# A fused attention and feed-forward kernel: the later pairs' queries and keys are split into high and low parts, stacked to 128 rows and projected with the whole array

## The chip, the core and the metric

The kernel runs on one core of one Trainium2 chip. The metric is the device time of one execution in microseconds (us); the time that stands for a kernel is the median of its timed runs. A difference under 0.2% of this kernel's time, some 2.3 us, is about what a measurement cannot tell from no change. Engines: PE (TensorE) runs the matmuls, PEld its weight loads, DVE is VectorE, ACT is ScalarE, POOL is GpSimd, SP is the queue from which nearly all transfers start.

## The reference

```python
def _attn_ref(q, k, v, w_phi):                       # q, k, v: 8 x 8 x 576 x 64, w_phi: 64 x 128
    def phi(x):
        proj = np.einsum('bhsd,df->bhsf', x, w_phi)
        proj = proj - np.max(np.abs(proj), axis=-1, keepdims=True)
        return np.concatenate([np.exp(proj), np.exp(-proj)], axis=-1)
    q_p, k_p = (phi(q), phi(k))
    kv = np.einsum('bhsf,bhsd->bhfd', k_p, v)
    z = np.sum(k_p, axis=2)
    num = np.einsum('bhsf,bhfd->bhsd', q_p, kv)
    den = np.einsum('bhsf,bhf->bhs', q_p, z)[..., None] + 1e-06
    return num / den

def _moe_ref(x, w_gate, w_val, w_out):               # x: 4608 x 512, inner width 1536
    g = x @ w_gate
    return (g * (1 / (1 + np.exp(-g))) * (x @ w_val)) @ w_out
```

The output of the attention, laid out as 4608 tokens by 512, is the x of the feed-forward part. All inputs are float32.

## The kernel before

**Work.** The 64 heads are 32 pairs of heads (`NPAIR` 4 to a batch entry, `i` counts them); the function `attention(i, rank)` adds one pair's steps. The first 12 pairs (`EARLY_PAIRS`) go through an early form, the other 20, called the later pairs here, through a second form. The tokens of the feed-forward part are 12 chunks of 384 (`CH`). The first 4 chunks use plain products (`first`, `second`), the other 8 are taken two at a time by Strassen's scheme (`operands`, `strassen`), whose operands are sums of quarters; those run from about 475 us on, and the first of them needs the later pairs' results.

**Precision.** Feed-forward products take float32 numbers as a high part, rounded to the type float32r, and a low part, the rest, and run three matmuls (high x high, high x low, low x high) in float32r; `matmuls` at line 389 and `prod` at line 1214 issue them, with 128 rows and 128 stationary columns each. The projections of attention use plain float32: one matmul of the program is two weight loads and two matmuls in the trace.

**Projection of a later pair.** A pair's keys lie as 64 rows for head 0 above 64 rows for head 1 in the tile `kin`, queries in `qin`, and `w_phi` lies twice, once for each half, in `wst`. A matmul takes 64 rows only, so the two heads' matmuls use the two halves of the array side by side (this is mode "rows" in the planner). For keys the tile of 128 tokens is stationary and `wst` moves; for queries `wst` is stationary and 288 tokens move:

```python
nc.tensor.matmul(work[plan.bank["k", i, h]][:, t * NF:(t + 1) * NF],          # 562
                 kin[rows(h)[0], t * P:(t + 1) * P], wst[rows(h)[0]], ...)
nc.tensor.matmul(work[plan.bank[keys[h]]][:, :SH], wst[rows(h)[0]],           # 705
                 qin[jq][rows(h)[0], c], ...)
```

Line 565 projects the last 64 tokens of both heads. What follows on keys (`L573`, `L579`, `L584`) makes their exponentials, `L601` and `L594` sum keys times values (called kv below), `L710` copies the queries out of PSUM, `L714` to `L742` make their exponentials, and `L760` multiplies them with the sums (called nu below). kv and nu use 64 columns of the array (mode "columns").

**Order.** Nothing is ordered by hand. Each step is added to a `Plan` with a cost, predecessors and a rank; `Plan.run` plays all engines forward with these costs, picks the next step of each engine, hands out the 8 PSUM banks, and issues in that order, so each engine's order is fixed when the kernel is built. `pe32(n)` is its cost for a pair of float32 projections, `pe(n)` for a float32r matmul, and 165 ns (`CHANGE`) are added where PE's mode changes. When PE has nothing ready, `nothing` issues an idle matmul of 128 x 256 (`L1413` and, before the feed-forward part begins, `L1411`).

**Weights.** `weight_piece` turns the float64 weights into high and low parts in 36 pieces, over scratch tiles `raw`, `we`, `wa`, which are slices of one tile `shared`. The later pairs' `turned` results reuse the room of `raw` when the weights are done.

Of the kernel before, what the change touches and what calls it, by code (L numbers as in the profile page):

```python
# [285 lines left out]
def favor_attention_moe(ctx: ExitStack, tc: tile.TileContext, qT, kT, v, w_phi, wg, wv, wo, out):  # L286
# [195 lines left out]

    turned = lambda n: later("turned", "shared", [P, 2, 2, 2, SH], F32)[:, n]

# [31 lines left out]
    def attention(i, rank):  # L516
# [8 lines left out]
        k_in = [add("SP", P * 4 * P * 4, lambda: nc.sync.dma_start(kin[:, :4 * P], kT[b, pr, :, :4 * P]),  # L525
                    [last.get(("kin", i - 1))], rank)]
        side = lambda t: t[:D, 4 * P:].rearrange("d (h s) -> d h s", h=2)
        ends = lambda t: t[b, pr, :, 4 * P:].rearrange("(h d) s -> d h s", h=2)
        k_in.append(add("SP", 2 * D * D * 4, lambda: nc.sync.dma_start(side(kin), ends(kT)), [last.get(("kin", i - 1))], rank))
        q_free = [last.get(("qin", n)) for n in ((i - 2,) if early else (i - 1, i - 2))]  # L530
        q_width = 4 * P if early else S
# [12 lines left out]

        kv_steps, summed, made_keys = [], [], []
        ps_kv = lambda: work[plan.bank["kv", i]]
        for g, (t0, t1) in enumerate(K_GROUPS):
# [9 lines left out]
            def project(t0=t0, t1=t1, key=key, heads=heads, both=both):  # L557
                projected.append(1)
                if not both:
                    for t in range(4):  # L560
                        for h in range(2):
                            nc.tensor.matmul(work[plan.bank["k", i, h]][:, t * NF:(t + 1) * NF],  # L562
                                             kin[rows(h)[0], t * P:(t + 1) * P], wst[rows(h)[0]], start=True, stop=True)
                if both or not early:
                    nc.tensor.matmul(work[plan.bank["k", i, 2]][:, :NF], kin[:D, 4 * P:], wst[:D], start=True, stop=True)  # L565

            if both and early:
                kproj = add("PE", pe32(NF), project, [*k_in, kproj], rank, take=key, mode="rows")
            elif not g:
                kproj = add("PE", (4 if early else 5) * pe32(NF), project, [*k_in, last.get(("kp", i - 1, 0))], rank,  # L570
                            take=[("k", i, n) for n in range(2 if early else 3)], mode="rows")
            m = km[(3 * i + g) % len(km)]
# [49 lines left out]
        last["kin", i] = kproj  # L622
        last["vf", i] = kv_steps[-1]
# [16 lines left out]
        if early:  # L640
            for g in range(3):
# [51 lines left out]
                f1 = add("ACT", act(size), lambda f=exponential: f(1), [f0, *([f1] if g else ())], rank, give=key2)  # L693
            last["qin", i] = pj
            if jq:
                ahead_used.append(pj)
        else:
            copies = [[], []]
            pj = None
            for part, c in enumerate(halves):  # L700
                keys = [("q", i, h, part) for h in range(2)]

                def project(keys=keys, c=c):
                    for h in range(2):
                        nc.tensor.matmul(work[plan.bank[keys[h]]][:, :SH], wst[rows(h)[0]], qin[jq][rows(h)[0], c],  # L705
                                         start=True, stop=True)

                pj = add("PE", pe32(SH), project, [*q_in, pj, *use("qx"), last.get(("qy", 3 * i - 1))], rank, take=keys, mode="rows")
                for h in range(2):
                    copies[h].append(add("ACT", act(SH), lambda h=h, part=part, key=keys[h]: nc.scalar.copy(  # L710
                        qx[j][:, h].rearrange("p (n u s) -> p u n s", u=2, s=32)[:, part],
                        work[plan.bank[key]][:, :SH].rearrange("p (n s) -> p n s", s=32)), [pj, *use("qx")], rank, give=keys[h]))
            last["qin", i] = pj
            turns = [add("DVE", dve(S), lambda h=h: vec.transpose(qe[j][:, h], qx[j][:, h]),  # L714
# [657 lines left out]
    for f in range(NFT):  # L1372
        sums(f)
    bring()
    behind = [(c, f) for c in (1, 2) for f in range(NFT)]
    coming.extend([*behind, *((PLAIN - 1, f) for f in range(NFT))])
# [89 lines left out]
```

## Time and profile before

| | |
|---|---|
| time, median of 3 runs | 1163.08 us (1162.91 to 1163.36) |
| the profiled execution, its own time | 1161.04 us |
| its span in the trace | 1159.2 us |
| busy PE | 1152.4 us, 99% |
| busy PEld | 1015.2 us, 88% |
| busy DVE | 793.7 us, 68% |
| busy ACT | 546.7 us, 47% |
| granted TensorE clock | full in every slice of the table |

Busy PE counts the overlapping, modelled ends of pipelined matmuls, and idle matmuls too, so 99% says that PE always has something in flight and not that it is at its peak. How long a matmul holds PE is read from a run of them: the time from the first to the start of what follows, divided by their number. The chain of waits lists PE that way. The DVE and ACT shares are means over stages that differ.

### The profile page before, as it was taken

Reading aid. Unit: us, or ns where it says so; the run is one execution under the profiler, and the core shown is the slowest. Engines: PE = TensorE matmul, PEld = TensorE weight load, DVE = VectorE, ACT = ScalarE, POOL = GpSimd, SP = SyncE. Lnnn points to the kernel's source line nnn. Section 1 sums busy time; section 2 is a strip of 40 time slices with the busy share of each in tenths; the row PEclk is TensorE's granted clock in tenths of the full one; section 3 lists DMA queues with packets and bytes.
Section 4 is the critical chain, followed back from the end, with each engine's and each line's share of the span. In section 5 each row is a group of like instructions: output and inputs, shape, how many; then the busy total and the mean of one; then the engine's idle time right before and its main releaser. Section 6 shows DMA issues by size and latency. Waiting matters only on the chain.

```text
span 1159.2 us, 26379 instructions
## 1 busy us (share of the span) xinstructions
PE 1152.4 (99%) x9985; PEld 1015.2 (88%) x9985; DVE 793.7 (68%) x1573; ACT 546.7 (47%) x1233; POOL 139.6 (12%) x142
## 2 busy tenths in 40 slices
PE   9999999999999999999999999999999999999998
PEld 8777779999898888898987899898899998899986
DVE  7989899999567777477787455777536786534431
ACT  6887563333434555445455343554423553433332
POOL 1222300000122313010010001100001100001100
PEclk9999999999999999999999999999999999999999
DMA  5546678777799999997887788887888787889774
GB/s 170 178 144 197 220 254 289 249 261 263 268 313 297 326 298 359 340 307 233 243 281 235 252 274 288 239 255 245 264 267 272 246 248 232 270 284 304 246 222 159
DMA packets 220591, 298.32 MB, mean 257 GB/s; under 512 B 65840, under 2 KB 126384, under 8 KB 220464
## 3 DMA queue, kind: packets, MB, share of 16 engines
q1 hardware_dynamic: 220304, 296.57, 79.7%
q8 instruction: 79, 1.29, 0.5%
q14 instruction: 48, 0.39, 0.1%
q10 hardware_dynamic: 160, 0.07, 0.0%
HBM read 217.91 MB, written 78.64 MB: 256 GB/s over the span
## 4 chain that ended last, share of the span: by engine, by line
PE 86%; DVE 1%; DMA 1%; issue 0%; SPq 0%; ACT 0%; ACTq 0%
PE work L389 41%; PE work L1214 31%; PE work L760 4%; PE work L601 4%; PE work L705 2%; PE work L562 2%; PE work L594 1%; PE work L1413 1%; DMA w_lo<-wlo_dram 0%; DMA stage<-x_dram 0%; PE work L565 0%; PE work L817 0%; PE work L813 0%; PE work L677 0%; DVE qy L667 0%
## 5 line engine op out<-in xcount | busy, mean ns | idle before, releaser
L389 PE MATMUL work<-w_hi,hh 128*128 128x512 f32 x468 | 183.1, 399 | 0.0
L1236 DVE TENSOR_TENSOR m<-m,work 128x384 f32<-128x384 f32 x144 | 78.6, 552 | 117.7 <-ACT m L1233 67.8
L389 PE MATMUL work<-w_hi,m 128*128 128x512 f32 x396 | 156.7, 396 | 0.0
L382 DVE TENSOR_TENSOR m<-m,hh 128x384 fp32r<-128x384 f32 x132 | 74.8, 573 | 97.7 <-ACT hh L1002 85.8
L1002 ACT CAST hh<-m 128x384 fp32r<-128x384 f32 x144 | 73.3, 512 | 138.5 <-PE work L389 74.2
L389 PE MATMUL work<-xh,w_big 128*128 128x384 f32 x384 | 132.3, 345 | 0.0
L382 POOL TENSOR_TENSOR m<-m,m 128x384 f32<-128x384 f32 x48 | 58.7, 1223 | 590.5 <-DVE m L1241 296.1
L389 PE MATMUL work<-xl,w_big 128*128 128x384 f32 x384 | 128.6, 335 | 0.0
L1214 PE MATMUL work<-tb,stream_xh 128*128 128x384 f32 x618 | 115.3, 338 | 0.0
L1214 PEld LDWEIGHTS work<-tb,stream_xh 128*128 128x128 f32 x618 | 107.0, 188 | 4.7 <-issue 3.8
L389 PEld LDWEIGHTS work<-w_hi,hh 128*128 128x128 f32 x468 | 87.9, 188 | 21.5 <-issue 1.7
L1233 ACT COPY m<-work 128x384 f32<-128x384 f32 x144 | 68.0, 475 | 73.2 <-PE work L1214 71.0
L1240 ACT ACTIVATE m<-m 128x384 f32<-128x384 f32 x96 | 45.5, 517 | 110.2 <-DVE m L1236 109.5
L584 ACT ACTIVATE kp<-kp 128x512 f32<-128x512 f32 x128 | 78.5, 630 | 26.5 <-DVE kp L579 25.3
L389 PEld LDWEIGHTS work<-w_hi,m 128*128 128x128 f32 x396 | 74.4, 188 | 17.8
L1214 PE MATMUL work<-tb,stream_xl 128*128 128x384 f32 x468 | 88.9, 338 | 0.4 <-ACT m L1233 0.4
L1214 PEld LDWEIGHTS work<-tb,stream_xl 128*128 128x128 f32 x468 | 81.0, 188 | 4.0 <-issue 2.3
L389 PEld LDWEIGHTS work<-xh,w_big 128*128 128x128 f32 x384 | 72.2, 188 | 7.5 <-issue 4.4
L1214 PE MATMUL work<-tb,tb 128*128 128x384 f32 x408 | 77.8, 337 | 0.0
L601 PEld LDWEIGHTS work<-vf,kp 128*64 128x64 f32 x2048 | 62.6, 138 | 13.4 <-issue 5.5
L382 POOL TENSOR_TENSOR s<-s 128x256 f32<-128x256 f32 x48 | 41.3, 862 | 270.1 <-DMA s<-w_dram 231.7
L389 PEld LDWEIGHTS work<-xl,w_big 128*128 128x128 f32 x384 | 72.2, 188 | 1.0
(141 smaller groups left out, 2340.1 us busy)
## 6 DMA issues: line engine op xcount, KB each, us to landing
stream_xh<-wv_dram SPq DMA_DIRECT2D x103, 256.0 KB, 4.0
h_dram<-m SPq DMA_DIRECT2D x124, 192.0 KB, 3.8
m<-h_dram SPq DMA_DIRECT2D x124, 192.0 KB, 4.1
stream_xl<-wv_dram SPq DMA_DIRECT2D x78, 256.0 KB, 3.9
tb<-wv_dram SPq DMA_DIRECT2D x77, 256.0 KB, 4.1
w_lo<-wlo_dram SPq DMA_DIRECT2D x72, 256.0 KB, 4.2
stream_w_lo<-wv_dram SPq DMA_DIRECT2D x52, 256.0 KB, 3.9
stream_xl<-wlo_dram SPq DMA_DIRECT2D x48, 256.0 KB, 3.8
```

The lines of the kernel that those rows point to most:

```text
L382: (nc.gpsimd if on == "POOL" else nc.vector).tensor_tensor(out=o, in0=a, in1=b, op=op)
L389: nc.tensor.matmul(o, l, r, start=a, stop=z)
L562: nc.tensor.matmul(work[plan.bank["k", i, h]][:, t * NF:(t + 1) * NF], kin[rows(h)[0], t * P:(t + 1) * P], wst[rows(h)[0]], start=True, st ...
L584: nc.scalar.activation(kpv[:, :m2, s], kpv[:, :m2, 1], AF.Exp, scale=-1.0 if s else 1.0)
L601: nc.tensor.matmul(ps_kv()[r, (2 * s + h) * VD:(2 * s + h + 1) * VD], kpv[:, t, s, r], vf[:, t, h], start=t == 0 and h + s == 0, stop=False)
L705: nc.tensor.matmul(work[plan.bank[keys[h]]][:, :SH], wst[rows(h)[0]], qin[jq][rows(h)[0], c], start=True, stop=True)
L760: nc.tensor.matmul(o[r, at:at + VD], features(k, h, slice(D * n, D * n + D)), kvs[j][:, (2 * k + h) * VD:(2 * k + h + 1) * VD], start=n % ...
L1002: s4 = add("ACT", act(CH), lambda: nc.scalar.copy(hh[b], th(j)), [made, hid_free[b]], FIRST)
L1214: nc.tensor.matmul(o(), l, r, start=begin and k + m == 0, stop=k + m == 3, skip_group_check=True)
L1233: return j, into(j, add("ACT", act(CH), lambda: nc.scalar.copy(th(j), src()), after, FIRST))
L1236: return add("DVE", dve(CH), lambda: vec.tensor_tensor(out=th(j), in0=th(j), in1=src(), op=ALU.add), after, FIRST)
L1240: s1 = into(t, add("ACT", act(CH), lambda: nc.scalar.activation(th(t), th(j), AF.Tanh, scale=0.5), [ready], FIRST))
```

## The change

The 20 later pairs' projections get another form. `w_phi` is split once into a high part `w_hi_phi` and a low part `w_lo_phi`. For each head of a later pair, ACT rounds the head's 64 rows to float32r into one half of a 128-row tile (`stack`), and DVE writes what is left over into the other half. One matmul over the 128 rows then multiplies high and low parts with `w_hi_phi`, a second adds their product with `w_lo_phi`. Each head's four key tiles fill one PSUM bank, and each half of a head's queries is a step with a bank of its own. The scratch tiles of the weights become six tiles, and the stacks take the room of `we` and `wa`.

```diff
+    w_parts = sb("w_hi_phi", [P, NF], F32R), sb("w_lo_phi", [P, NF], F32R)
...
-    shared = pool.tile([P, 4, 2 * DM], F32, name="shared", tag="shared")
-    shared = [shared[:, i].bitcast(dt) for i, dt in enumerate((U32, U32, F32, F32))]
-    raw = [t.rearrange("p (n t) -> p n t", t=2) for t in shared[:2]]
-    we, wa = ([t[:, i * DM:(i + 1) * DM] for i in range(2)] for t in shared[2:])
+    raw = [t[:, :2 * DM].rearrange("p (n t) -> p n t", t=2) for t in sb("raw", [P, 2 * S], U32, 2)]
+    we = [sb("we0", [P, 4 * P])[:, :DM], sb("we1", [P, S])[:, :DM]]
+    wa = [sb("wa0", [P, KW])[:, :DM], sb("wa1", [P, S])[:, :DM]]
...
+    STACKS = {"k1": ("we0", 4 * P), "q0": ("we1", S), "k0": ("wa0", KW), "q1": ("wa1", S)}
...
+    def split_phi():
+        hi = add("ACT", act(NF), lambda: nc.scalar.copy(w_parts[0], wst), (), EARLY_PAIRS - 0.5)
+        phi_parts.append(add("DVE2", dve(NF), lambda: nc.vector.tensor_tensor(
+            out=w_parts[1], in0=wst, in1=w_parts[0], op=ALU.subtract), [hi], EARLY_PAIRS - 0.5))
+    def stacked(name, h, src, n, after, rank):
+        own, other = rows(h)
+        free = [*wa_free, *we_free]
+        hi = add("ACT", act(n), lambda: nc.scalar.copy(stack(name)[own, :n], src[own, :n]), [*after, *free], rank)
+        return [hi, add("DVE2", dve(n), lambda: nc.vector.tensor_tensor(
+            out=stack(name)[other, :n], in0=src[own, :n], in1=stack(name)[own, :n], op=ALU.subtract), [hi], rank)]
...
+            def project_whole(g=g, t0=t0, t1=t1, key=key, both=both):
+                projected.append(1)
+                for t in range(t0, t1) if both else range(4):
+                    o = work[plan.bank[key]][:, :NF] if both else work[plan.bank[key]][:, t * NF:(t + 1) * NF]
+                    for n, w in enumerate(w_parts):
+                        nc.tensor.matmul(o, stack("k0" if both else f"k{g}")[:, t * P:(t + 1) * P], w, start=n == 0, stop=n == 1)
+            if not early:
+                kproj = add("PE", (1 if both else 4) * 2 * pe(NF), project_whole,
+                            [*key_parts[g % 2], *phi_parts, last.get(("kp", i - 1, g))], rank, take=key)
...
-                pj = add("PE", pe32(SH), project, [*q_in, pj, *use("qx"), last.get(("qy", 3 * i - 1))], rank, take=keys, mode="rows")
+                    def project(h=h, at=at, ps_q=ps_q):
+                        for n, w in enumerate(w_parts):
+                            nc.tensor.matmul(ps_q(), w, stack(f"q{h}")[:, at], start=n == 0, stop=n == 1)
+                    pj = add("PE", 2 * pe(SH), project, [*parts_of[h], *phi_parts, *use("qx"), last.get(("qy", 3 * i - 1))],
+                             rank, take=key)
```

What this does to the issued order is seen at three places. The first is PE in the first Strassen stage, at a later pair's queries. Before (L705 the query projections, two heads side by side; L1214 feed-forward products):

```order
L705 MATMUL work_131<-qin,wst 128x288
L705 MATMUL work_134<-qin,wst 128x288
L1214 MATMUL work_127<-tb_4973,stream_xh_5354 128x384 x6
L1214 MATMUL work_133<-tb_5018,stream_xh_5041 128x384 x3
L705 MATMUL work_130<-qin,wst 128x288
L705 MATMUL work_132<-qin,wst 128x288
L1214 MATMUL work_133<-tb_5018,stream_xh_5041 128x384 x3
```

In the change, at the like place (L740 the new query projections, L1248 the former L1214):

```order
L1248 MATMUL work_136<-tb_5168,stream_w_lo1v 128x384 x3
L740 MATMUL work_139<-stack_q_3458,w_hi_phi 128x288
L740 MATMUL work_139<-stack_q_3458,w_lo_phi 128x288
L1248 MATMUL work_136<-tb_5168,stream_w_lo1v 128x384 x3
L740 MATMUL work_137<-stack_q_3458,w_hi_phi 128x288
L740 MATMUL work_137<-stack_q_3458,w_lo_phi 128x288
L1248 MATMUL work_140<-tb_5261,tb_5252 128x384 x6
```

Two steps of two 64-row matmuls became four steps of two 128-row matmuls, each between products. In the whole order the later pairs' 80 matmuls of L705 become 160, and their 180 of L562 and L565 become 360 of a new line 591; the idle matmuls of L1413 go from 67 to 56; all feed-forward matmuls are the same in number.

The second place is PE where a later pair's kv (L601, L594) and another's nu (L760) stand, in the same stage. Before:

```order
L1214 MATMUL work_129<-tb_4973,stream_xh_5041 128x384 x6
L601 MATMUL work_131<-vf,kp_101 64x65 x16
L601 MATMUL work_131<-vf,kp_102 64x65 x16
L594 MATMUL work_131<-vl,kpt 64x130 x4
L760 MATMUL work_134<-kvs_104,qe_108 64x65 x2
L760 MATMUL work_134<-kvs_104,qx_106 64x65 x2
```

In the change (L631 and L624 are kv, L794 is nu):

```order
L631 MATMUL work_134<-vf,kp_103 64x65 x16
L631 MATMUL work_134<-vf,kp_104 64x65 x16
L624 MATMUL work_134<-vl,kpt 64x130 x4
L1248 MATMUL work_140<-tb_5252,stream_w_lo1v 128x384 x6
L1248 MATMUL work_136<-tb_5168,tb_5252 128x384 x6
L1248 MATMUL work_140<-tb_5261,tb_5252 128x384 x6
L794 MATMUL work_139<-kvs_106,qe_110 64x65 x2
```

Products of 128 columns now stand between the two. Counted over the 20 later pairs, kv and nu stand next to each other 14 times before and 6 times in the change. Of the 40 steps of L705 before, 34 have products on both sides and 6 stand next to another attention block; the 20 key blocks stand apart from kv and nu.

The third place is DVE in the same stage, behind the subtraction of the query maxima (L738 before, L772 in the change). Before:

```order
L735 STREAM_TRANSPOSE qe_108<-peaks 128x576 x2
L738 TENSOR_TENSOR qx_106<-qx_106,qe_108 128x576 x2
L573 TENSOR_REDUCE km_113<-work_131 128x4
L573 TENSOR_REDUCE km_114<-work_134 128x4
L579 TENSOR_TENSOR kp_101<-work_131,km_113 128x4x128
L1236 TENSOR_TENSOR m_5898<-m_5898,work_133 128x384
```

In the change (L499 are the new low parts, L1270 is the former L1236):

```order
L772 TENSOR_TENSOR qx_109<-qx_109,qe_111 128x576
L499 TENSOR_TENSOR stack_k_3431<-kin,stack_k_3431 64x640
L499 TENSOR_TENSOR stack_k_3439<-kin,stack_k_3439 64x512
L499 TENSOR_TENSOR stack_q_3445<-qin,stack_q_3445 64x576
L499 TENSOR_TENSOR stack_q_3458<-qin,stack_q_3458 64x576
L772 TENSOR_TENSOR qx_109<-qx_109,qe_111 128x576
L1270 TENSOR_TENSOR m_5705<-m_5705,work_135 128x384
```

All four subtractions of a pair stand together here, ahead of L1270, which empties PSUM banks of the products; elsewhere they come one or two at a time.

## Rows read from the trace of the kernel before

**Rows 1.** The page: engines, busy us, share of the span, instructions.

```profile
PE 1152.4 (99%) x9985; PEld 1015.2 (88%) x9985; DVE 793.7 (68%) x1573; ACT 546.7 (47%) x1233; POOL 139.6 (12%) x142
```

**Rows 2.** Chain of waits, long runs: start us, us, what.

```profile
460.13 2.75 PE work L1413 x23
...
999.97 17.48 PE work L389 x75
1017.45 85.48 PE work L1214 x492
```

**Rows 3.** Chain of waits in the first Strassen stage: start us, us, what.

```profile
541.14 2.10 PE work L760 x72
543.24 1.79 PE work L1214 x9
545.02 0.69 PE work L705 x4
545.71 1.79 PE work L1214 x9
547.50 0.69 PE work L705 x4
548.18 4.91 PE work L1214 x27
553.09 1.09 PE work L562 x16
554.18 0.22 PE work L565 x2
554.40 10.63 PE work L1214 x60
565.03 2.02 PE work L601 x64
567.04 0.44 PE work L594 x8
567.49 2.10 PE work L760 x72
569.59 1.79 PE work L1214 x9
```

**Rows 4.** Chain of waits at 414 us: a nu block alone.

```profile
414.62 2.25 PE work L760 x72
```

**Rows 5.** Timeline of PEld behind mode changes: start us, us, operation, count.

```profile
482.97 0.30 PEld L1214 LDWEIGHTS work<-tb,stream_w_lo 128*128 128x128 f32 x2
```

**Rows 6.** Groups by line and form: count, busy us, mean ns of one, idle before.

```profile
L1214 PEld LDWEIGHTS work<-tb,stream_xh 128*128 128x128 f32 x618 | 107.0, 188 | 4.7 <-issue 3.8
...
L738 DVE TENSOR_TENSOR qx<-qx,qe 128x576 f32<-128x576 f32 x40 | 29.8, 773 | 0.0
...
L740 ACT ACTIVATE qe<-qx 128x576 f32<-128x576 f32 x40 | 27.0, 683 | 11.6 <-DVE qx L738 11.2
...
L430 ACT CAST w_big<-shared 128x512 fp32r<-128x512 f32 x24 | 14.9, 621 | 15.5 <-DVE shared L382 15.2 <-POOL shared L382 0.2
...
L382 DVE TENSOR_TENSOR w_lo<-shared,w_hi 128x512 fp32r<-128x512 f32 x7 | 4.8, 687 | 0.0
```

**Rows 7.** Windows, three stretches with later pairs: busy us and instructions of each engine.

```profile
480.00:600.00 120.00, 120.00 (x1316) 108.53 (x1316) 88.24 (x184) 60.30 (x141) 12.39 (x10) 1.00 0.85 271
720.00:800.00 80.00, 80.00 (x882) 72.44 (x881) 64.18 (x133) 42.64 (x97) 8.46 (x7) 1.00 0.85 259
880.00:960.00 80.00, 80.00 (x780) 72.38 (x780) 60.05 (x123) 40.78 (x95) 9.08 (x8) 1.00 0.80 249
```

**Rows 8.** Windows of line 562 alone: PE and PEld busy us (records, 16 for a pair).

```profile
480.00:600.00 120.00, 6.97 (x96) 5.83 (x96) 1.00 0.85 271
720.00:800.00 80.00, 3.49 (x48) 2.91 (x48) 1.00 0.85 259
```

**Rows 9.** Tile `shared`: engine, operation, count, ns min/median/max, first and last start us.

```profile
L430 ACT CAST w_hi<-shared x12: 603/622/629, 62.9 to 295.2; 128x512 fp32r<-128x512 f32 x12
```

**Rows 10.** Chain of waits: the keys of the first two later pairs.

```profile
187.48 1.09 PE work L562 x16
...
342.25 1.09 PE work L562 x16
```

More of the change, by code (lines that the diff above doesn't have):

```diff
@@ L545, in attention @@
         kv_steps, summed, made_keys = [], [], []
+        if not early:
+            key_parts = [stacked(f"k{h}", h, kin, (KW, 4 * P)[h], [*k_in, *last.get(("keys", i - 1, h), ())], rank) for h in range(2)]
         ps_kv = lambda: work[plan.bank["kv", i]]
@@ L563, in project @@
                                              kin[rows(h)[0], t * P:(t + 1) * P], wst[rows(h)[0]], start=True, stop=True)
-                if both or not early:
+                if both:
                     nc.tensor.matmul(work[plan.bank["k", i, 2]][:, :NF], kin[:D, 4 * P:], wst[:D], start=True, stop=True)
-            if both and early:
+            def project_whole(g=g, t0=t0, t1=t1, key=key, both=both):
[4 more added lines that the diff above has]
+                        nc.tensor.matmul(o, stack("k0" if both else f"k{g}")[:, t * P:(t + 1) * P], w, start=n == 0, stop=n == 1)
+            if not early:
+                kproj = add("PE", (1 if both else 4) * 2 * pe(NF), project_whole,
+                            [*key_parts[g % 2], *phi_parts, last.get(("kp", i - 1, g))], rank, take=key)
+                last.setdefault(("keys", i, g % 2), []).append(kproj)
+            elif both:
                 kproj = add("PE", pe32(NF), project, [*k_in, kproj], rank, take=key, mode="rows")
             elif not g:
-                kproj = add("PE", (4 if early else 5) * pe32(NF), project, [*k_in, last.get(("kp", i - 1, 0))], rank,
-                            take=[("k", i, n) for n in range(2 if early else 3)], mode="rows")
+                kproj = add("PE", 4 * pe32(NF), project, [*k_in, last.get(("kp", i - 1, 0))], rank,
+                            take=[("k", i, n) for n in range(2)], mode="rows")
             m = km[(3 * i + g) % len(km)]
@@ L621, in attention @@
                 last["kp", i, g] = kv_steps[0]
-        last["kin", i] = kproj
+        last["kin", i] = [kproj] if early else [key_parts[h][1] for h in range(2)]
         last["vf", i] = kv_steps[-1]
@@ L693, in attention @@
                 f1 = add("ACT", act(size), lambda f=exponential: f(1), [f0, *([f1] if g else ())], rank, give=key2)
-            last["qin", i] = pj
+            last["qin", i] = [pj]
             if jq:
@@ L698, in attention @@
             copies = [[], []]
[L699 to L706, printed above, removed]
-                pj = add("PE", pe32(SH), project, [*q_in, pj, *use("qx"), last.get(("qy", 3 * i - 1))], rank, take=keys, mode="rows")
-                for h in range(2):
-                    copies[h].append(add("ACT", act(SH), lambda h=h, part=part, key=keys[h]: nc.scalar.copy(
+            parts_of = [stacked(f"q{h}", h, qin[jq], S, [*q_in, *last.get(("stack", i - 1, h), ())], rank) for h in range(2)]
+            last["qin", i] = [parts_of[h][1] for h in range(2)]
+            for h in range(2):
+                last["stack", i, h] = []
+                for part in range(2):
+                    at = slice(part * SH, part * SH + SH)
+                    key = ("q", i, h, part)
+                    ps_q = lambda key=key: work[plan.bank[key]][:, :SH]
+                    def project(h=h, at=at, ps_q=ps_q):
[3 more added lines that the diff above has]
+                             rank, take=key)
+                    last["stack", i, h].append(pj)
+                    copies[h].append(add("ACT", act(SH), lambda h=h, part=part, ps_q=ps_q: nc.scalar.copy(
                         qx[j][:, h].rearrange("p (n u s) -> p u n s", u=2, s=32)[:, part],
-                        work[plan.bank[key]][:, :SH].rearrange("p (n s) -> p n s", s=32)), [pj, *use("qx")], rank, give=keys[h]))
-            last["qin", i] = pj
+                        ps_q().rearrange("p (n s) -> p n s", s=32)), [pj, *use("qx")], rank, give=key))
             turns = [add("DVE", dve(S), lambda h=h: vec.transpose(qe[j][:, h], qx[j][:, h]),
@@ L1374, in favor_attention_moe @@
     bring()
+    split_phi()
     behind = [(c, f) for c in (1, 2) for f in range(NFT)]
```

10 lines of the change are left out of this document (6 added, 4 removed).

## The prediction

> **What bounds the kernel now.** I read the page first, then the chain of waits, then groups and windows. The page shows PE in flight for 99% of the span and no other engine above 68% [rows 1]; this says only where to look, since a busy PE may be issuing idle matmuls or waiting for its weights. The chain tells what a matmul costs in a run. 492 feed-forward matmuls of 128 x 384 take 85.48 us, 0.1737 each; 75 of 128 x 512 take 17.48 us, 0.233 each; 23 idle ones of 128 x 256 take 2.75 us, 0.1196 each [rows 2]. In the Strassen stage products and attention blocks follow each other without a break: the run of 60 products behind a key block takes 10.63 us, and 60 times 0.1737 is 10.42 [rows 3]. The 0.2 us left over stands in every such run between two attention blocks (9 products take 1.79 where 9 times 0.1737 is 1.56), however long the run, so it is the price of leaving and entering the 128 x 128 mode, and not a wait. What PE waits is in its order as idle matmuls: 67 of L1413 at 0.12 are 8.0 us. So the time is the sum of PE's work, and the change is priced as PE's work.
>
> **Removed.** A key block is 1.09 + 0.22 us (L562, L565), from 553.09 to 554.40, plus the 0.2 of its mode change: 1.51 us. One step of queries is 0.69 us, with its mode change 0.89 [rows 3]. Of the 40 steps 34 stand between products and cost 0.89; 6 share the mode change with a neighbour and cost 0.69. The 20 pairs: 20 x 1.51 + 34 x 0.89 + 6 x 0.69 = 30.2 + 30.3 + 4.1 = 64.6 us.
>
> **Added on PE.** 160 matmuls with 288 moving columns and 360 with 128, all in the mode of the products, so without a mode change. For 288 the rows at 256 and 384 give 0.133 by a straight line [rows 2]: 160 x 0.133 = 21.3 us. For 128 moving columns in float32r on the whole array no row exists, and this is the price that decides. From below: the same straight line gives 0.066. But each matmul has a weight load of its own (9985 of each, [rows 1]), and behind a mode change, where nothing holds back the second load, two loads in a row take 0.30 us [rows 5]. One load is 0.188 [rows 6], so the second begins 0.11 us after the first: a load of 128 columns holds its path for 0.11 us. The products at 0.17 and the idle ones at 0.12 hide that; 128 moving columns don't. From above: a plain float32 matmul of this size costs 0.22 us (the two records of L565, [rows 3]). I take 0.11, which is read from loads of the very shape that is added: 360 x 0.11 = 39.6 us.
>
> On this point the Trainium skill has a figure ("TensorE: Matmul & The Clock Gate", section "Back-to-back issue gap"): in a stream of loads and matmuls 128 moving columns sustain about 81 ns each and 512 about 131 ns. No run here has shown the first; the second differs from this trace, where 512 columns take 233 ns [rows 2], so I give the first little weight. With 0.081 in place of 0.11 the sum below would be lower by 10.4 us, which is a rival below.
>
> **Moved on PE.** kv alone is 565.03 to 567.49, 2.46 us, and 0.2 for the mode: 2.66. nu alone is 2.25 + 0.2 = 2.45 [rows 4]. Together they are 2.46 + 2.10 + 0.2 = 4.76 [rows 3], since they share the mode of 64 columns. Each pair of them that is parted costs 2.66 + 2.45 - 4.76 = 0.35 us. Neighbours fall from 14 to 6: 8 x 0.35 = 2.8 us more. The idle matmuls fall by 11: 1.3 us less.
>
> **Added on ACT and DVE.** A pair gets four casts and four subtractions, of 512, 640 and twice 576 columns. 512 costs 0.621 on ACT and 0.687 on DVE, 576 costs 0.683 and 0.773 [rows 6]; one more step of 64 gives 0.745 and 0.859 for 640. That is 2.73 us of ACT and 3.09 us of DVE for a pair, 55 and 62 us in all. Both engines have the room: with 62 us more DVE is at 74% of the span, ACT at 52% [rows 1]. It is hidden behind PE's products. In the fullest stretch, 720 to 800 us, DVE has 64.2 of 80 busy [rows 7] with 3 pairs' keys [rows 8]; 9.3 more make 73.5, or 92%; in 480 to 600 us 6 pairs bring it from 88.2 to 106.8 of 120, or 89%. So the cover is thin there. I count nothing for it in the sum and up to 1.5 us in the bounds; without the cover it is the second rival below.
>
> **Waits that are new.** The new PE steps wait for DVE's low part; queued behind them on PE are feed-forward products. The stacks wait until the weights' scratch is free, that is about 297 us (the last rounding starts at 295.2 [rows 9]; with its 0.62 and a subtraction of 0.69 behind it, 296.5). Before, the first later pair's keys were projected at 187 us; now they come behind the weights. The second was at 342 us [rows 10], so only one pair is moved, into a stretch that held its other steps. `kin` and `qin` are free when DVE has subtracted and no longer when PE has projected, which lets their loads start earlier; nothing waited for them in the rows of the chain, so that is worth nothing. SP has no more transfers than before. Splitting `w_phi` is one cast and one subtraction of 128 columns at the start, under 1 us, while the first pair's keys are still being projected: nothing. The six scratch tiles in place of one leave the early pairs' order as it was: nothing.
>
> **Sum.** 39.6 + 21.3 + 2.8 - 1.3 - 64.6 = -2.2 us. Against the profiled execution's own 1161.04 us (span 1159.2 and 1.8 around it) that is 1158.8; the median of the runs lies 2.0 above that execution, at 1163.08, so the forecast for the median is **1160.9 us**. The (20 + 34) x 0.2 = 10.8 us of mode changes that are saved are eaten by weight loads: a pair's keys cost 18 x 0.11 = 1.98 us in place of 1.51, its queries 8 x 0.133 = 1.06 in place of about 1.72.
>
> **Rivals.**
> 1. *The load is no bound.* If 128 moving columns cost what the straight line gives, 0.066, PE's added work falls by 360 x 0.044 = 15.8 us: 1145.1. By the Trainium skill's figure above it would be 1150.5. For it: the straight line fits three lengths within 0.01 us. Against it: rows 5, and that no matmul in those rows of this mode is quicker than 0.12.
> 2. *DVE holds PE up (slower).* Four subtractions stand together in DVE's order, 3.09 us, ahead of the additions that empty the products' banks. PE waits if the products' banks come free late; the loss turns the result when it passes 2.2 us in all, 0.11 us a pair, and shows as slower beyond 0.2% from 4.5 us, 0.23 a pair. With half a subtraction exposed for each pair (0.39 us, 7.7 in all) the time is 1168.6. For it: 92% of DVE in a stretch. Against it: the planner put fewer idle matmuls into PE's order than before, with a cost of 0.749 us for a DVE step of 576 columns (`dve`: 150 + 1.04 n ns) against 0.773 in the rows; and it reckons a new key matmul at 0.063 (`pe`: 7 + 0.441 n) where I take 0.11, so that PE comes later than planned and DVE has more time.
> 3. *Short float32r matmuls run like plain float32 (slower).* At 0.22 for 128 columns the sum rises by 360 x 0.11 = 39.6 us: 1200.5. For it: nothing in the trace shows float32r under 256 columns. Against it: at 256 a float32r matmul has one record and takes 0.12, and nothing in the rows falls off towards shorter ones.
>
> That the change doesn't do what it says is no rival: the order shows the matmuls exchanged, one for one as counted.
>
> **How the numbers follow.** The forecast case has 0.70; rival 1 has 0.12, rival 2 0.11, rival 3 0.07. In the forecast case the load may be 0.105 to 0.115 (1.8 us each way) and DVE may cost up to 1.5: its own range is 1158.6 to 1164.5. The bound of 0.2%, 2.3 us, which is about what a measurement can tell, runs at 1160.75, through the middle of it: 0.31 faster, 0.37 the same, 0.02 slower. Rival 1 is faster, rival 3 slower, rival 2 slower by 0.09 and the same by 0.02. In all: faster 0.43, same 0.39, slower 0.18. The range leaves out rivals 1 and 3 (0.19) and reaches to rival 2: 1157 to 1169.
>
> **What would show it.** In the profile after, 18 matmuls of a key block in a run should take 1.9 to 2.05 us in the chain, a query step of two 0.27, and no 0.2 us should stand in the product runs beside them. PEld should be busy without a break in the key blocks. kv and nu blocks keep their 2.46 and 2.1 to 2.25 us. The groups should show DVE's 80 subtractions at about 0.69 to 0.86 us. The forecast is wrong if a key block takes 1.2 us (rival 1) or 4 us (rival 3), or if product runs in 480 to 600 or 720 to 800 us lengthen by waits for DVE (rival 2).

## The result, and the profile after

The changed kernel takes 1171.6 us (median of 5 runs, 1170.5 to 1171.9), the kernel before 1162.9 in the same comparison: a ratio of 1.0075, 95% interval 1.0062 to 1.0089. It is slower by 8.7 us, and the time lies above the forecast range. The profiled execution took 1171.15 us, with a span of 1169.4. One execution of experiment 9 took 1808 us at a granted clock of 0.58 and is left out of its time; it is the only one of that kernel with a trace.

The page of the changed kernel, the row that answers to [rows 1]:

```profile
PE 1155.4 (99%) x9974; PEld 1043.2 (89%) x9974; DVE 866.6 (74%) x1654; ACT 596.4 (51%) x1314; POOL 139.4 (12%) x142
```

DVE has 73 us more, ACT 50, and PE is "99%" as before: the page does not show what went wrong. The chain of waits in a stretch of the Strassen stage that answers to [rows 3]:

```profile
736.43 1.76 PE work L1248 x9
738.20 1.96 PE work L591 x18
740.16 0.59 PE work L1248 x3
740.75 0.27 PE work L740 x2
741.01 1.59 PE work L1248 x9
742.60 0.80 PE work L740 x6
743.41 5.24 PE work L1248 x30
748.65 2.02 PE work L631 x64
750.66 0.44 PE work L624 x8
```

Here everything is as forecast. A block of 18 key matmuls takes 1.96 us (forecast 1.98), two query matmuls 0.27, kv 2.46, and the 9 products between them 1.59, without the 0.2 of a mode change. The groups by line and form show the new steps of DVE and ACT (count, busy us, mean ns):

```profile
L499 DVE TENSOR_TENSOR stack_q<-qin,stack_q 64x576 fp32r<-64x576 f32 x40 | 33.5, 838 | 1.9 <-ACT stack_q L498 0.7
...
L499 DVE TENSOR_TENSOR stack_k<-kin,stack_k 64x640 fp32r<-64x640 f32 x20 | 18.6, 930 | 2.4 <-ACT stack_k L498 1.9
...
L499 DVE TENSOR_TENSOR stack_k<-kin,stack_k 64x512 fp32r<-64x512 f32 x20 | 17.8, 888 | 0.5
```

That is 69.9 us of DVE where 62 were forecast. The loss itself is seen in windows of the changed kernel (busy us of PE, PEld, DVE, ACT and POOL, then the granted clock, the DMA share and GB/s). The window from 187 to 1100 us holds all later pairs:

```profile
187.00:1100.00 913.00, 905.36 (x7307) 841.36 (x7306) 677.86 (x1305) 450.65 (x956) 96.20 (x93) 1.00 0.85 272
```

The same window of the kernel before:

```profile
187.00:1100.00 913.00, 912.56 (x7376) 823.40 (x7375) 610.35 (x1234) 404.08 (x882) 97.55 (x94) 1.00 0.85 273
```

PE is idle for 0.4 us before and for 7.6 after. The table of what PE waited for in the change (line, releaser, us in total, times, longest):

```profile
PE work L794 <- ACT qe L774: 3.0, 2, 2.6
PE work L740 <- DVE kp L609: 2.0, 1, 2.0
PE work L389 <- DVE m L382: 1.3, 2, 1.0
PE work L1248 <- ACT m L1267: 0.5, 2, 0.3
PE work L794 <- ACT qx L776: 0.4, 1, 0.4
```

The first two and the last belong to one place, at the start of the Strassen stage. Windows of it, first the kernel before, then two of the change:

```profile
480.00:520.00 40.00, 40.00 (x418) 36.23 (x419) 26.90 (x55) 19.78 (x47) 3.84 (x4) 1.00 0.96 324
```

```profile
480.00:520.00 40.00, 34.53 (x319) 32.96 (x316) 34.57 (x68) 23.23 (x48) 2.47 (x2) 0.91 0.87 289
...
498.00:504.00 6.00, 3.91 (x52) 3.34 (x54) 5.69 (x13) 5.90 (x12) 0.00 (x0) 0.50 0.95 320
```

PE idles 5.47 of 40 us (before: none). It idles 2.0 us up to 495.5 and 2.6 us up to 499.2, and the granted clock falls to the lower of its two levels: 0.50 from 498 to 504 us. The nu block there runs into it. The chain of waits at that place:

```profile
483.19 0.63 ACT s L1128
...
483.85 0.56 DVE s L382 x2
...
484.52 0.75 DVE s L382 x2
...
485.31 0.82 DVE stack_k L499
...
486.15 1.02 DVE m L1270 x2
...
491.31 1.45 DVE stack_q L499
...
492.79 0.75 DVE stack_q L499
493.55 1.21 DVE km L603 x2
...
494.78 1.29 DVE kp L609 x2
...
497.81 0.65 DVE qx L772
...
498.48 0.68 ACT qe L774
...
500.21 1.27 ACT qx L776 x2
```

In place of a row of PE's runs the chain leaves PE at 482.8 us and returns at 501.5. It goes through one pair's keys and queries on DVE and ACT, and at its head stand `s L1128` and `s L382`: the last of the 12 sums of weights (`sums`) that the Strassen products multiply with. They stand in this chain because DVE does them just ahead of that pair's low parts. In between PE has nothing but 46 products up to 491.1 us and this pair's keys, queries and nu. The last of these products in the timeline, and the next in the chain:

```profile
487.94 3.28 PE L1248 MATMUL work<-tb,tb 128*128 128x384 f32 x18
```

```profile
507.39 2.28 PE work L1248 x12
```

For some 16 us no product starts; in the kernel before the hole between the same products is 3.6 us (489.4 to 493.1). The timeline of SP shows what the next products needed, the last stores of the sums and a load of weights behind them:

```profile
491.66 1.19 SPq L1133 DMA_DIRECT2D wv_dram<-s  x2
...
497.99 0.43 SPq L1182 DMA_DIRECT2D stream_xh<-wv_dram  x1
```

The second store starts at 492.4 us and takes 4.7 us to land. The load starts 0.9 us after that; by the order of the loads in the code it is the first into a room that the sums had held. In the kernel before the same load starts 4.6 us after the last store has landed. The profile names no wait for it, and seven other transfers stand between stores and load in SP's order, so the rows show the sequence and not which of the two held the load.

**Where all of it went.** An account of PE from 187 us on, from the start of each matmul to the start of the next: each is booked with the usual distance of its kind (0.173 us for 384 columns, 0.233 for 512, 0.111 for the new keys, 0.1325 for the new queries, and the like), and what is over that by more than 40 ns is a wait. In us:

| | before | after | sums_first | queries_sums_first |
|---|---|---|---|---|
| projections of the later pairs and mode changes | 69.8 | 67.7 | 67.6 | 56.8 |
| kv and nu | 92.1 | 95.7 | 93.5 | 92.8 |
| idle matmuls | 7.9 | 6.6 | 8.8 | 8.1 |
| waits | 1.3 | 12.9 | 8.7 | 3.9 |
| products, with small deviations | 796.7 | 794.9 | 795.1 | 796.4 |
| sum | 967.8 | 977.7 | 973.7 | 957.9 |

Without the waits the sum falls from 966.5 to 964.8 us, by 1.7 where 2.2 were forecast, and that holds 1.5 us which the nu block lost at the lower clock. The loss is in the waits: 11.6 us more, and of the 12.9 there are 6.4 between 480 and 520 us.

### The profile page after: what moved, and what is told of

The parts are those of the page before. It is cut to its first block, busy times and chain, and to the rows that moved or that the text cites. A ratio compares the mean times of both kernels' runs of the same rounds, so it can differ in the third digit from the quotient of the medians.

```text
span 1169.4 us, 26553 instructions
## 1 busy us (share of the span) xinstructions
PE 1155.4 (99%) x9974; PEld 1043.2 (89%) x9974; DVE 866.6 (74%) x1654; ACT 596.4 (51%) x1314; POOL 139.4 (12%) x142
## 4 chain that ended last, share of the span: by engine, by line
PE 82%; DVE 5%; ACT 1%; issue 1%; DMA 0%; SPq 0%; DVEq 0%; ACTq 0%
PE work L389 40%; PE work L1248 28%; PE work L794 4%; PE work L631 3%; PE work L591 3%; PE work L740 2%; PE work L624 1%; PE work L1448 1%; DVE s L382 0%; DVE m L1270 0%; DVE qe L769 0%; PE work L851 0%; DVE stack_k L499 0%; DVE stack_q L499 0%; DVE kp L609 0%
## 5 line engine op out<-in xcount | busy, mean ns | idle before, releaser
L1270 DVE TENSOR_TENSOR m<-m,work 128x384 f32<-128x384 f32 x144 | 78.0, 550 | 100.8 <-ACT m L1267 57.9
L382 DVE TENSOR_TENSOR m<-m,hh 128x384 fp32r<-128x384 f32 x132 | 73.0, 561 | 77.8 <-ACT hh L1036 75.1
L382 POOL TENSOR_TENSOR m<-m,m 128x384 f32<-128x384 f32 x48 | 59.0, 1229 | 581.7 <-DVE m L1275 363.6
L1248 PE MATMUL work<-tb,stream_xh 128*128 128x384 f32 x618 | 116.0, 337 | 0.3 <-ACT m L1267 0.3
L1248 PEld LDWEIGHTS work<-tb,stream_xh 128*128 128x128 f32 x618 | 106.8, 188 | 1.5 <-issue 0.7
L1248 PE MATMUL work<-tb,stream_xl 128*128 128x384 f32 x468 | 89.4, 336 | 0.2 <-ACT m L1267 0.2
L1248 PEld LDWEIGHTS work<-tb,stream_xl 128*128 128x128 f32 x468 | 80.9, 188 | 0.9 <-ACT m L1267 0.5
L1248 PE MATMUL work<-tb,tb 128*128 128x384 f32 x408 | 78.1, 336 | 0.2 <-DVE m L1270 0.2
L382 POOL TENSOR_TENSOR s<-s 128x256 f32<-128x256 f32 x48 | 40.9, 854 | 289.1 <-DMA s<-w_dram 232.0
L631 PEld LDWEIGHTS work<-vf,kp 128*64 128x64 f32 x2048 | 62.7, 138 | 14.1 <-issue 5.6
```

Source lines behind the costliest of these rows:

```text
L382: (nc.gpsimd if on == "POOL" else nc.vector).tensor_tensor(out=o, in0=a, in1=b, op=op)
L631: nc.tensor.matmul(ps_kv()[r, (2 * s + h) * VD:(2 * s + h + 1) * VD], kpv[:, t, s, r], vf[:, t, h], start=t == 0 and h + s == 0, stop=False)
L1248: nc.tensor.matmul(o(), l, r, start=begin and k + m == 0, stop=k + m == 3, skip_group_check=True)
L1270: return add("DVE", dve(CH), lambda: vec.tensor_tensor(out=th(j), in0=th(j), in1=src(), op=ALU.add), after, FIRST)
```

## The experiments

Three theories. **A**: it is the amount of new work on DVE (70 us) and ACT. **B**: it is the order that the planner makes around the new query projections and the nu blocks behind them. **C**, formed from the chain above after the first four runs: the sums of the weights come late. They share a priority with the later pairs' steps, whose number the change raises; the first stage's products load their weights into rooms that the sums' tiles hold (in `stream`, a load into the rooms `xh2` and `xl2` waits for `sums_made[-6:]`, the last sums' stores), so with late sums the products are not ready, and PE has only one pair's chain left to run.

**1. short_low: DVE's work taken out, order kept.** Each low part after the first use of its tile is written for 32 columns only; the rest of the tile keeps an older low part.

```diff
+        w = n if name not in late else 32
+        late.setdefault(name)
...
-            out=stack(name)[other, :n], in0=src[own, :n], in1=stack(name)[own, :n], ...
+            out=stack(name)[other, :w], in0=src[own, :w], in1=stack(name)[own, :w], ...
```

> The changed kernel in its own order on every engine, but DVE's subtractions into the stacks cover 32 columns only after a tile's first use (the low parts of later pairs are left out; everything else is computed). That takes about 2.3 us of DVE from each later pair, 45 us in all. Theory A, PE waits because the added DVE work delays what PE needs: the waits of PE behind DVE at 360 to 380 us and 484 to 502 us go, and the time falls to the sum of PE's work, 1161 to 1163 us. Theory B, the waits come from the order (the planner put a nu block and query projections behind each other with no products between): they stay within 2 us of what they are and the time is 1168 to 1172 us.

Measured: 1169.9 us, ratio 1.0052 (1.0037 to 1.0067). The 80 subtractions take 25.0 us in its trace in place of 69.9, and of some 9 us only 1.7 come back (2.7 by the ratios). PE still idles 4.6 us between 480 and 520. As far as DVE goes, theory A can be no more than a small part; ACT's casts, 50 us, were left in here and in every other run.

**2. more_slack.** The planner keeps more distance ahead of PE's steps in the due times.

```diff
-    SLACK = {"PE": 1500, "ACT": 300, "DVE": 300}
+    SLACK = {"PE": 6000, "ACT": 300, "DVE": 300}
```

> The changed kernel with one constant of the planner raised: a PE step of the pairs from the 17th on counts as ready 6.0 us after its inputs and no longer 1.5 us. All work is the same. In the order every nu block then stands behind products; kv and nu are neighbours once and no longer 6 times, which costs 5 x 0.35 = 1.8 us, and there are 2 idle matmuls fewer. Theory A (amount of DVE work): DVE's load is unchanged, so PE still waits and the time stays at 1168 or above. Theory B (order): PE has products to do while DVE and ACT finish the queries, the waits go, and the time is 1162 to 1164 us.

Measured: 1168.6 us, 1.0044 (1.0027 to 1.0060); 3.3 us idle at 480 to 520. Theory B's 1162 to 1164 did not come. The chain of waits at this place, now with another end:

```profile
490.63 1.78 PE work L1248 x9
...
492.64 5.28 DMA tb<-wv_dram
...
497.94 4.64 DMA stream_xh<-wv_dram
...
502.62 5.48 PE work L1248 x21
```

PE's products now wait for the loads of their weights themselves. The load of `stream_xh` starts at 497.9 us, 7 us behind the last store of a sum (`wv_dram<-s` at 490.7). That store takes 4.9 us to land, and the last wait that the chain names for the load is another load, `tb<-wv_dram`. That the load has to wait for the store is read from the code (theory C) and not from these rows; they show that loads of weights are what is late here.

**3 and 4. queries_alone, keys_alone.** The change for one of the two kinds only, the other as before.

> Only the queries are stacked; the keys go back to the 64-row float32 form. PE's work by the rows: queries 21.3 in place of 34.4 us, 5 partings of kv and nu 1.8, 3 more idle matmuls 0.4, together -11.0 us against the kernel before, so 1152 us without waits. The order still has one place where query projections, nu and kv follow without products. Theory A: DVE gets half of the added work, half of the waits stay: about 1156. Theory B: the place stays, so the wait there stays whole: about 1160.

> Only the keys are stacked; the queries go back to the 64-row float32 form. PE's work by the rows: keys 360 x 0.111 = 40.0 in place of 30.2 us, 8 partings of kv and nu 2.8, 36 idle matmuls fewer -4.3, so about +8.5 us against the kernel before: 1171 us without waits. Theory A: half of the waits on DVE come on top: about 1175. Theory B: waits where nu stands behind query projections (one such place in the order): 1173 to 1179.

Measured: the queries alone 1157.8 us, 0.9950 (0.9935 to 0.9965), faster than before; the keys alone 1170.5, 1.0057 (1.0041 to 1.0074). The queries lie between the two theories (1156 and 1160), the keys below both and at the sum without waits (1171). The queries alone idle 4.0 us at 480 to 520, the keys alone none: the late sums come with the queries, whereas the keys cost on PE itself.

**5. sums_first.** The test of theory C: the sums get a priority ahead of the later pairs' steps. In `Plan.run` the edit does a second thing: transfers of a rank above 11.6 are held back while the planned queue is full, and at 11.6 the sums' are not. The arithmetic stays; the order changes, and with it the idle matmuls, 74 in place of 56.

```diff
-        vec, rank = nc.vector, 11.9
+        vec, rank = nc.vector, 11.6
```

> The change as it is, but the sums of the weights (the 12 steps whose results the first stage's products multiply with) get a priority of 11.6 instead of 11.9, so that they stand ahead of the later pairs' steps. The arithmetic and the number of instructions are the same. Theory C (the waits of 12.9 us are at bottom late sums: the last of them is stored at 485.6 to 492.4 us in the changed kernel, at 471.7 to 475.2 us before, and TensorE's stage behind it runs dry at 484 to 508 us): the last store moves to 479 us or earlier, the waits between 484 and 508 us fall from about 7 to under 3 us, and the time falls by 4 to 8 us, to 1163 to 1168 us. Theory A (it is the amount of VectorE's and ScalarE's work, which is unchanged here): 1169 to 1173 us. Theory B (it is the order around the nu blocks behind the query projections): 1169 to 1173 us, since these steps keep their priority.

Measured: 1166.8 us, 1.0039 (1.0025 to 1.0053), 4.8 less than the change. The last sums' stores in the trace of the changed kernel (count, issue ns, first and last start in 440 to 500 us):

```profile
L1133 SPq DMA_DIRECT2D wv_dram<-s x4: 371/503/676, 468.6 to 492.4; - x4
L1136 SPq DMA_DIRECT2D wv_dram<-s x3: 370/371/577, 444.5 to 485.6; - x3
```

and with the sums first:

```profile
L1133 SPq DMA_DIRECT2D wv_dram<-s x6: 378/414/477, 441.2 to 474.5; - x6
L1136 SPq DMA_DIRECT2D wv_dram<-s x3: 370/384/442, 444.7 to 475.0; - x3
```

The window of sums_first at this place (columns as above):

```profile
480.00:520.00 40.00, 38.84 (x292) 37.51 (x291) 37.17 (x74) 26.36 (x59) 3.75 (x3) 1.00 0.97 324
```

The last store moves from 492.4 to 475.0, the idle time from 5.5 to 1.2, and the clock stays full. DVE is fuller here than in the change (37.17 of 40 against 34.57), and PE still hardly waits; ACT is fuller too (26.36 against 23.23). So it is not the load of either that stops PE there. This is theory C's forecast, in the place and in the time.

**6. before_sums_first, the control.** The same edit in the kernel before.

> The kernel before, with the same priority of 11.6 for the sums of the weights. A control: it tells how much of what the sums' priority gives has to do with the change. Theory C: in the kernel before the sums were in time, or cost little (its waits of over 0.2 us add up to 1.3 us), so the time stays within 2 us of the kernel before, 1161 to 1165 us. If the sums' priority is worth as much here as in the changed kernel (4 us and more, under 1160 us), then it is a general gain and says nothing of the change.

Measured: 1160.4 us, 0.9979 (0.9969 to 0.9988), 0.6 below theory C's range. The priority is worth 2.5 us even without the change, so about half of the 4.8 us is general. By the ratios it is 4.2 us with the change and 2.4 without, and the intervals leave open whether the two differ. This limits theory C: it explains the place of the largest wait, and not the whole loss.

**7. queries_sums_first.** Queries alone and sums first.

> Only the queries are stacked (the keys are projected as before), and the sums of the weights have a priority of 11.6. The queries alone gave 1157.8 us with waits of 8.3 us and a last store at 482.0 to 482.6 us. Theory C: the last store comes at 470 us or earlier, the waits fall by 3 to 6 us, and the time is 1152 to 1155 us. Theories A and B: no change to the queries alone, 1157 to 1159 us.

Measured: 1150.3 us, 0.9895 (0.9880 to 0.9910), better than either theory said, and the fastest kernel here. Its chain of waits in the Strassen stage:

```profile
570.61 0.54 PE work L734 x4
571.15 0.53 PE work L1242 x3
571.68 0.53 PE work L734 x4
572.22 1.58 PE work L1242 x9
573.79 1.09 PE work L579 x16
574.88 0.22 PE work L582 x2
575.10 10.12 PE work L1242 x57
```

The query steps (L734) stand between products (L1242) without a mode change, 3 products in 0.53; the keys (L579, L582) keep their cheap old form of 1.31. In the window of 480 to 520 us PE is busy throughout:

```profile
480.00:520.00 40.00, 40.00 (x414) 38.66 (x412) 22.93 (x45) 15.78 (x36) 5.00 (x4) 1.00 0.97 331
```

**8. honest_price.** A rival that the runs might have hidden, theory D: the planner counts a new key matmul at 63 ns where it takes 111, and so plans too much behind it.

```diff
-    return max(58, 7 + 0.441 * n)
+    return max(111, 7 + 0.441 * n)
```

> The change as it is, but the planner's smallest price of one of TensorE's matmuls is 111 ns instead of 58 ns, which is what one of the new key projections takes in the trace of the changed kernel. It changes only the order. A theory D (the planner fills too much work in behind the key projections because it counts them at about half of their time, and that is why TensorE waits): the waits fall from 12.9 us to under 6 us and the time is 1162 to 1166 us. Theory C: the price has nothing to do with the sums; the last store stays at 485 us or later, and the time stays at 1168 us or above.

Measured: 1167.4 us, 1.0043 (1.0028 to 1.0058). The time lies between the two forecasts, but by the account the waits are 12.0 us instead of 12.9, not under 6; 4.6 us at 480 to 520 stay. The last store came at 482.0, earlier than theory C said. So the wrong price is not what makes PE wait; the new order lost less in the nu blocks (44.6 us in the account instead of 46.9), with a granted clock of 0.96 at 480 to 520 us in place of 0.91. But it gains 4.2 us by order alone, nearly as much as sums_first: the time does not tell the theories apart, the idle time at this place does.

**9. sums_first_short.** Experiment 1 on top of 5, with the low parts of most columns left as they were.

> sums_first with its order kept, and each later subtraction for the low parts cut to 32 columns after the first use of its tile, so that some 53 us of VectorE's work are left out (the low parts of most columns then stay as they were). The waits that sums_first still has are 8.7 us, of which 2.2 at 480 to 520 us. If these are VectorE coming late (what is left of theory A), the time falls by 3 to 6 us, to 1161 to 1164 us. If they stand in the order that was planned (theories B and C), by less than 2 us, 1165 to 1167 us.

Measured: 1166.4 us, 1.0033 (1.0021 to 1.0044). By the traces the subtractions take 23.7 us in place of 68.0, so 44 us were left out and not the 53 that were expected. That gives 0.4 us: what sums_first still waits is not DVE's amount either.

**10. keys_sums_first.** The last corner of the square.

> Only the keys stacked, and the sums of the weights at priority 11.6. It completes the square with before_sums_first (1160.4), queries_sums_first (1150.3) and sums_first (1166.8). The keys alone cost 6.8 us at the old priority, where their sums were stored by 470.0 us, earlier than in the kernel before, and their waits were 3.4 us. Theory C: the sums were in time already, so the new priority gives at most 3 us, 1167.5 to 1171 us; what the keys cost is TensorE's own work (40.0 us for 26.0, less 2.4 of mode changes). If the keys' loss is a matter of the order, the time falls under 1165 us.

Measured: 1172.2 us, 1.0084 (1.0068 to 1.0099), 1.2 above the range of theory C, although PE waits little (3.2 us in the account, none at 480 to 520). Medians in us:

| | neither | queries | keys | both |
|---|---|---|---|---|
| sums at 11.9 | 1162.9 | 1157.8 | 1170.5 | 1171.6 |
| sums at 11.6 | 1160.4 | 1150.3 | 1172.2 | 1166.8 |

With the sums in time, queries gain 10.2 us and keys cost 11.8; together they cost 6.4, 4.8 more than the two apart. The new priority itself is worth 2.5, 7.5, -1.7 and 4.8 us in the four columns.

**11. queries_sums_slack.** Experiment 7 with the slack of 2.

> Only the queries stacked, the sums of the weights at priority 11.6, and a larger slack for TensorE in the planner (6000 in place of 1500 ns), to see whether the 3.9 us of waits that queries_sums_first still has can be planned away. Theory C: the waits were mostly settled by the sums, so 0 to 2 us more are to be had, 1148 to 1151 us; with the slack as the cause of what is left, below 1148 us.

Measured: 1151.3 us, 0.9904 (0.9889 to 0.9919): no gain over experiment 7.

**12. low_parts_apart.** Why were the sums late? Part of a sum's work is GpSimd's, and the planner keeps steps marked "DVE2" apart from GpSimd's. Here the subtractions are unmarked.

```diff
-        return [hi, add("DVE2", dve(n), lambda: nc.vector.tensor_tensor(
+        return [hi, add("DVE", dve(n), lambda: nc.vector.tensor_tensor(
```

> The change as it is, but the planner counts the stacks' subtractions as ordinary VectorE steps and not as ones that may not run beside GpSimd's (its rule is that such steps and GpSimd's steps exclude each other). Only the order changes. It asks why the sums, part of whose work is GpSimd's, became late. If it is this exclusion that pushed them back: the last sum is stored at 484 us or earlier instead of 492.4, the waits at 480 to 520 us fall from 6.4 to under 4 us, and the time is 1164 to 1168 us, less what the subtractions lose beside GpSimd. If the sums are late for another reason (their loads, or ScalarE's share): the last store stays at 489 us or later and the time at 1169 to 1173 us.

Measured: 1169.6 us, 1.0057 (1.0040 to 1.0074). The last store moved to 484.2, the idle time at 480 to 520 only to 3.9 us, and the time stayed in the range of the other answer. So without the exclusion the sums come some 8 us earlier, and that alone is not enough to have the products ready; what the other 9 us of their delay come from was not found.

**The runs side by side**, by the start of the last sum's store and PE's idle time between 480 and 520 us:

| kernel | last store, us | PE idle, us |
|---|---|---|
| keys_sums_first | 446.1 | 0 |
| before_sums_first | 457.2 | 0 |
| queries_sums_slack | 466.8 | 0 |
| queries_sums_first | 468.3 | 0 |
| keys_alone | 470.0 | 0 |
| sums_first | 475.0 | 1.2 |
| before | 475.2 | 0 |
| honest_price | 482.0 | 4.6 |
| queries_alone | 482.6 | 4.0 |
| low_parts_apart | 484.2 | 3.9 |
| more_slack | 490.7 | 3.3 |
| short_low | 492.1 | 4.6 |
| after | 492.4 | 5.5 |

It reads like a threshold: up to 475 us PE has products and idles 1.2 us at most, from 482 us on it idles 3 to 6 us, whatever the theory that a kernel was made for. The times do not follow it alone. keys_sums_first stores earliest and takes longest, and each of the four other orders of the whole change is faster than its own, by 2.0 to 4.8 us, even more_slack (3.0), whose sums are nearly as late. So part of what sums_first gains may come with any new order, and that rival stands.

## Why the prediction was wrong

**PE's work: right.** Keys at 0.111 us a matmul (forecast 0.11), queries at 0.1325 (0.133), kv and nu blocks of their old length, mode changes gone: 67.7 us of projections and mode changes for 69.8. The sum of -2.2 was right as a sum of PE's work (-1.7 in the account). Its own range, 1158.6 to 1164.5, is a little wider than its terms give, 1159.1 to 1164.2; that changes nothing here. Rivals 1 and 3 fell with it. By the Trainium skill ("TensorE: Matmul & The Clock Gate", section "Back-to-back issue gap") 128 moving columns would sustain about 81 ns; the trace does not agree, at 111.

**The step that failed is "What PE waits is in its order as idle matmuls", and with it "So the time is the sum of PE's work".** It was read from a kernel with 0.4 us of idle time and made into a rule; in the change the waits are 12.9 us in the account where they were 1.3. In the code, `nothing` issues an idle matmul only while no product has begun or a sum is open in PSUM (`elif open_sum`); otherwise it returns the time and issues nothing. In the changed kernel PE idles 7.6 us with 56 idle matmuls in place of 67. I counted the fall of 11 idle matmuls as a gain of 1.3 us, but an order can hold waits without an idle matmul to show them.

**"So the cover is thin there. I count nothing for it in the sum and up to 1.5 us in the bounds" failed as well, but otherwise than rival 2 had it.** I looked for the cover in DVE's busy share. At 480 to 520 us PE ran dry where its products' weights came late: with the added steps the last sum of the weights is stored 17 us later, and with the sums ahead the idle time there falls from 5.5 to 1.2 us. Rival 2 (DVE holds PE up, 1168.6) named the engines that stand in the chain at that place, but its mechanism, a queue of subtractions, is worth 0.4 to 1.7 us in the runs that took the subtractions out. Its price came near by accident. The forecast listed which transfers, buffers and PE steps the change touches, and left out which other steps stand in the same priority class as the added ones.

**The lower clock.** It was not in any case of the prediction. It costs about 1.5 us: the nu block that [rows 4] show at 2.25 us took 3.50 for 65 of its 72 matmuls, where 65 in the old time are 2.03.

**The two halves.** From the prediction's own terms the queries alone would have come to 21.3 - 34.4 = -13.1 us and the keys alone to 39.6 - 30.2 = +9.4. With the sums in time they measured -10.2 and +11.8. I added them up without saying that one half is a gain and the other a loss; that was the most useful thing the terms had to tell.

**What stays open.** Of the 8.7 us that sums_first waits, 1.1 stand between two plain products right behind the first later pair's keys, at 309 us, 2.2 at 480 to 520, and the rest in pieces of up to 0.8 us over the whole run. They are not DVE's amount (experiment 9); that they come from the planned order is what is left, and was only argued. Even with its sums in time the change takes 1166.8 us, above the forecast's own range; so the late sums are at most about half of the loss, and the other half has no cause that a run shows. Nor is it settled why queries and keys together cost 4.8 us more than apart, beyond that waits (2.0) and idle matmuls (3.2) account for it: in the account, waits are 0.4, 3.9, 3.2 and 8.7 us and idle matmuls 6.6, 8.1, 4.1 and 8.8 for neither, queries, keys and both.

## What to carry to other kernels

In a kernel ordered by a planner, adding work to one class of steps can delay the other steps of that class (the last sum by 17 us with both parts, by 7 with the queries alone, not at all with the keys alone); so look for who shares the priority, and whose buffers the critical engine's next loads wait for, before counting off-path work at nothing. A busy share of 99% with no idle time says that the present order works, and not that the next one will. Price the parts of a change one by one: here the one with 288 moving columns gained and the one with 128, whose matmuls go at the pace of the weight loads, lost, and the part with a gain, with the weights' sums moved ahead, is 1.05% faster than before.

## What the runs showed of the hardware

**DVE's subtraction beside GpSimd.** The times of the 80 subtractions fall into two groups. By the records of the changed kernel, 61 have no GpSimd instruction beside them and take 686 to 821 ns, none over 1000; of the 19 that overlap one, 17 take 1.0 to 1.64 us. One of them in the timeline, on GpSimd and then on DVE (start us, us; the second row holds two subtractions, of which the first took 1.45):

```profile
490.94 1.21 POOL L382 TENSOR_TENSOR m<-m,m 128x384 f32<-128x384 f32 x1 [12.42 <-PE work L1248]
```

```profile
491.31 2.24 DVE L499 TENSOR_TENSOR stack_q<-qin,stack_q 64x576 fp32r<-64x576 f32 x2
```

GpSimd's addition ran beside it for 0.84 us, and it lost 0.70. The 19 together take 9.7 us more than they would alone, which is more than the 8 us by which the forecast for DVE was short. The Trainium skill ("SBUF — State Buffer", section "Who interferes with whom") says that a VectorE instruction with two inputs in SBUF contends with a GpSimd instruction that reads SBUF; the trace agrees, with 0.75 us alone and 1.45 beside it, for 17 of the 19.

**128 columns go at the pace of the load.** The key matmuls follow each other at 0.109 to 0.111 us, the distance that [rows 5] showed between two weight loads in a row, while 288 columns take 0.1325: 2.25 times the columns for 1.2 times the time. That the load is the bound is inferred from the equal distances; no run changed the load alone.
